# Two of thirty V loads cut into a 112-row transfer and sixteen loose rows from GpSimd's queue

## The chip, the core and the metric

One core of one Trainium2 chip runs the kernel. The core has five engines that work side by side: TensorE (PE, matrix products), VectorE (DVE), ScalarE (ACT), GpSimd (POOL) and SyncE (SP), which here only issues transfers. Data come from HBM into SBUF, the on-chip memory of 128 partitions, through 16 DMA engines that all issuing queues share. The metric is the device time of one execution in microseconds, lower is better; several executions are timed and their median is taken.

## The reference

One decode step of a gated mix: a grouped-query attention over a cached sequence of 65,536 keys, a small token-mixing network, and a gate between the two. What matters here is the attention, since it reads 536.9 MB of cache (8 heads x 65,536 x 256 x 2 bytes, for K and for V).

```python
def _A_ref(x, k_cache, v_cache, wq, wo):          # x [1,1,448], caches [1,8,65536,256], bf16
    q = (x @ wq).reshape(B, Sq, 16, 256)          # 16 query heads, two to each K/V head
    k = repeat(k_cache, 2, axis=1); v = repeat(v_cache, 2, axis=1)
    scores = einsum("bhqd,bhkd->bhqk", q, k) * 256 ** -0.5
    o = einsum("bhqk,bhkd->bhqd", softmax(scores), v)
    return o.reshape(B, Sq, 16 * 256) @ wo
g = sigmoid((x * gate_w).sum(-1))
out = g * _A_ref(...) + (1 - g) * _B_ref(...)     # _B_ref: layernorm, 448 x 1792 gelu network
```

## The kernel before

The cache is walked in 32 blocks, n = 0 to 31: four blocks of 16,384 positions for each of the 8 heads. In a block, partition p holds 128 neighbouring positions, so a row (one partition's share) of K or V is 128 x 256 numbers, 64 KB, and is contiguous in HBM.

Three buffers hold cache data. K of a block lies in two tiles, `kn0` and `kn1` (`k_tiles`, L79), each 128 rows of 32 KB; V lies in one tile `vt` (L80), 128 rows of 64 KB. There is no second copy of any of them: the next transfer into a buffer can begin only when the last reader of its old contents is done and the transfer before it into that buffer has landed.

A block does the following. `score_block` (L355) turns K around on TensorE (`transposes`, L332, four matrix transposes to a PSUM bank, then a copy by VectorE at L337) and multiplies it with the query (`scores`, L346). `softmax` (L394) takes the running maximum and exponentials. `products` (L490) multiplies the weights with V: four calls of `pv` (L369), one for each 32 of the 128 positions of a row, 16 matmuls each (L373), so calls 0 and 1 read the first half of each row of `vt` and calls 2 and 3 the second half. `accumulate` adds the result into `acc`.

All large loads are issued by SP, in program order: in block n first V of this block (`load_v`, L115, called at L527), then the two halves of K of the next block (`load_k`, L108). Each is one transfer of 128 rows. SP waits at V(n) until `products(n-1)` has read `vt`, and at each K half until `score_block(n)` has read that tile. `seq` (L58) keeps every engine's instructions in the order of the program; it orders only within an engine. GpSimd does four small things at the start of the kernel and nothing after that. Blocks 30 and 31 load V in smaller pieces, which the change leaves alone.

Names used below: V10 is V of block 10; K10a and K10b are the two halves of K of block 10. `KP` is 64, half of the 128 positions of a row; `VP` is 128.

## Time and profile before

| what | value |
|---|---|
| median of 3 timed runs | 1282.58 us (1281.82 to 1283.41) |
| the profiled execution's own time | 1282.07 us |
| its span, first to last instruction | 1280.3 us |
| PE busy | 980.6 us, 77% |
| DVE busy | 753.9 us, 59% |
| ACT, POOL busy | 43.0 us, 4.2 us |
| moved by DMA | 545.54 MB, mean 426 GB/s |
| issue to landing, K half (63 of them) | 26.8 us median |
| DVE's copy of a transposed K piece (L337) | 1024 x 0.685 us |
| TensorE's product with V (L373) | 1920 x 0.536 us |

The profile is one execution. A busy share says how much of the span an engine worked, not whether anything waited for it; the chain of waits and the waits of the issuing queue say that. The time from issue to landing counts what is still queued ahead of a transfer as well as its own time. The trace also keeps a record of every DMA packet with start, duration, size and queue, but not with the number of the DMA engine that carried it.

### The profile page before, as it was taken

The page shows a single profiled execution, that of the slowest core. Times are in us where ns is not written, and L with a number is a line of the kernel's source. Part 1 is how long each engine was busy: PE and PEld are TensorE (multiplying, and loading weights), DVE is VectorE, ACT ScalarE, POOL GpSimd, SP SyncE. Part 2 cuts the span into 40 slices and gives each one's busy share as a digit, 9 for nine tenths or more (in the row PEclk, how much of TensorE's full clock was granted, in tenths as well). Part 3 has the DMA queues.
Part 4 walks back from the last instruction along what each step waited for, and adds up shares of the span by engine and source line. Part 5 has one row for each costly group of instructions (what it writes and reads, how often), then busy time and mean ns, then how long its engine had stood idle before and what let it go on. Part 6 is the DMA issues. An engine that isn't in the chain of part 4 may idle for free.

```text
span 1280.3 us, 20506 instructions
## 1 busy us (share of the span) xinstructions
PE 980.6 (77%) x8941; PEld 643.2 (50%) x8941; DVE 753.9 (59%) x1368; ACT 43.0 (3%) x109; POOL 4.2 (0%) x7
## 2 busy tenths in 40 slices
PE   5777677787778787777876677866879777797797
PEld 4455444554545555445544455544456444565475
DVE  5465556664557655566654566644676545675573
ACT  4000000000000000000000000000000000000000
POOL 1000000000000000000000000000000000000000
PEclk9888878897888978889988889888888878897896
DMA  9999999999999999999999999999999999999897
GB/s 408 425 435 425 441 419 436 429 437 428 447 418 433 440 438 429 424 431 432 438 436 424 437 424 437 431 437 432 426 433 433 443 416 426 433 428 434 387 416 294
DMA packets 17716, 545.54 MB, mean 426 GB/s; under 512 B 2136, under 2 KB 4186, under 8 KB 4698
## 3 DMA queue, kind: packets, MB, share of 16 engines
q1 hardware_dynamic: 17188, 544.22, 98.8%
q8 instruction: 70, 1.15, 0.3%
q14 instruction: 20, 0.16, 0.0%
q10 hardware_dynamic: 438, 0.01, 0.0%
HBM read 544.22 MB, written 0.00 MB: 425 GB/s over the span
## 4 chain that ended last, share of the span: by engine, by line
DMA 67%; PE 30%; DVE 2%; issue 0%
DMA kn<-in_A_k_cache_dram 67%; PE tps L332 23%; PE sc_ps L346 5%; DVE kT L337 1%; PE pv_ps L387 1%; PE hd_ps L387 1%; DMA xr<-in_A_x_dram 0%; PE tps L589 0%; PE tps L554 0%; DVE rmax L398 0%; DVE z L280 0%; PE sm_ps L407 0%; DVE zt L279 0%; PE sm_ps L560 0%; PE sm_ps L496 0%
## 5 line engine op out<-in xcount | busy, mean ns | idle before, releaser
L337 DVE COPY kT<-tps 128x1024 bf16<-128x1024 bf16 x1024 | 646.5, 685 | 176.2 <-PE tps L332 175.2
L332 PE MATMUL tps<-ident_f,kn 128*128 128x128 f32 x4096 | 601.9, 296 | 99.7 <-DMA kn<-in_A_k_cache_dram 99.7
L332 PEld LDWEIGHTS tps<-ident_f,kn 128*128 128x128 f32 x4096 | 485.4, 150 | 219.1 <-DMA kn<-in_A_k_cache_dram 112.1
L373 PE MATMUL pv_ps<-vt,pT 128*4 128x512 bf16 x1920 | 172.1, 536 | 95.3 <-DMA vt<-in_A_v_cache_dram 89.5
L346 PE MATMUL sc_ps<-kT,qpad 128*32 128x512 bf16 x2048 | 201.1, 393 | 28.1 <-DVE kT L337 27.9
L373 PEld LDWEIGHTS <-pT 128*4 128x4 bf16 x1920 | 57.3, 110 | 197.4 <-issue 138.7
L439 DVE SCALAR_TENSOR_TENSOR acc<-acc,al,pv_ps 128x512 f32<-128x512 f32 x22 | 16.5, 748 | 163.0 <-PE pv_ps L373 163.0
L346 PEld LDWEIGHTS <-qpad 128*32 128x32 bf16 x2048 | 53.0, 93 | 110.7 <-issue 102.4
L416 ACT ACTIVATE p_sb<-sc_ps,nb 128x512 bf16<-128x512 f32 x32 | 22.0, 687 | 1205.5 <-DVE nb L410 1100.0
L444 DVE COPY acc<-pv_ps 128x512 f32<-128x512 f32 x8 | 5.5, 692 | 59.2 <-PE pv_ps L373 59.2
L429 DVE STREAM_TRANSPOSE pT<-p_sb 128x512 bf16<-128x512 bf16 x32 | 22.8, 711 | 28.3 <-ACT p_sb L416 28.3
L398 DVE TENSOR_REDUCE rmax<-sc_ps 128x1 f32<-128x512 f32 x32 | 22.1, 692 | 23.0 <-PE sc_ps L346 23.0
L399 PE MATMUL sm_ps<-ident_f,rmax 128*1 128x128 f32 x32 | 8.7, 271 | 25.4 <-DVE rmax L398 25.4
L407 PE MATMUL sm_ps<-mrun,ones_f 1*128 1x2 f32 x64 | 14.2, 288 | 14.1 <-DVE mrun L406 11.7
L399 PEld LDWEIGHTS sm_ps<-ident_f,rmax 128*1 128x1 f32 x32 | 2.5, 79 | 41.3 <-DVE rmax L398 41.3
L407 PEld LDWEIGHTS sm_ps<-mrun,ones_f 1*128 1x128 f32 x64 | 11.4, 221 | 20.2 <-DVE mrun L406 16.3
L410 DVE CUSTOM_DVE_ANT_0 junk<-sm_ps,nval 128x2 f32<-128x2 f32 x32 | 5.1, 159 | 17.1 <-PE sm_ps L407 17.1
L447 PE MATMUL hd_ps<-lsum,same 128*128 128x1 f32 x14 | 4.1, 362 | 13.9 <-DVE lsum L431 13.9
L447 PEld LDWEIGHTS hd_ps<-lsum,same 128*128 128x128 f32 x14 | 3.5, 310 | 14.5 <-DVE lsum L431 14.5
L400 DVE TENSOR_REDUCE mnew<-sm_ps 1x2 f32<-1x64 f32 x24 | 5.1, 212 | 8.7 <-PE sm_ps L399 8.7
L237 ACT ACTIVATE wo_sb<-h_bc,b1f,w1f 128x448 bf16<-128x448 f32 x14 | 9.2, 748 | 5.3 <-DVE h_bc L232 5.3
L461 PE MATMUL hd_ps<-esc,acc 128*128 128x2 f32 x28 | 4.4, 263 | 6.0 <-DVE acc L439 6.0
(107 smaller groups left out, 135.5 us busy)
## 6 DMA issues: line engine op xcount, KB each, us to landing
kn<-in_A_k_cache_dram SPq DMA_DIRECT2D x63, 4096.0 KB, 26.8
vt<-in_A_v_cache_dram SPq DMA_DIRECT2D x1, 5120.0 KB, 27.1
kn<-in_A_k_cache_dram SPq DMA_DIRECT2D x2, 2048.0 KB, 12.2
kn<-in_A_v_cache_dram SPq DMA_DIRECT2D x1, 4096.0 KB, 18.4
wo_sb<-in_A_wo_dram SPq DMA_DIRECT2D x1, 3584.0 KB
vt<-in_A_wq_dram SPq DMA_DIRECT2D x1, 3072.0 KB, 10.0
vt<-in_A_v_cache_dram SPq DMA_DIRECT2D x1, 3072.0 KB
kn<-in_A_v_cache_dram SPq DMA_DIRECT2D x1, 2048.0 KB, 17.9
```

Source lines behind the costliest of these rows:

```text
L237: seq(nc.scalar.activation(out=gel[:, b, :], in_=h_bc[:], func=ACT.Gelu_apprx_tanh, scale=w1f[:, b:b + 1], bias=b1f[:, b:b + 1],))
L332: seq(nc.tensor.transpose(tp[:, jj * 128:(jj + 1) * 128], k_tiles[i // 4][:, i % 4 * NJ + quarter * 4 + jj, :].bitcast(FP32), ident_f[:, :],))
L337: seq(nc.vector.tensor_copy(out=kT_tiles[i % 2][:, quarter * 4:(quarter + 1) * 4, :, :].rearrange("p j n c -> p (j n c)"), in_=tp[:, :].bi ...
L346: seq(nc.tensor.matmul(sc_ps[32 * a:32 * (a + 1), :], lhsT=qpad[:, c, g, i, :], rhs=kT_tiles[i % 2][:, :, 32 * a:32 * (a + 1), c], start=( ...
L373: seq(nc.tensor.matmul(pv_ps[32 * grp:32 * grp + 2 * REP, :, :], lhsT=pT[:, 32 * jj + 2 * REP * ip:32 * jj + 2 * REP * (ip + 1)], rhs=pair ...
L387: seq(nc.tensor.matmul(dst[:, c, :], lhsT=tile(j).rearrange("p (d c) -> p c d", c=2)[:, c, :], rhs=pT_tiles[v][:, 32 * jj + REP * i:32 * j ...
L398: seq(nc.vector.tensor_reduce(out=rmax[:], in_=sc_ps[:, :], op=ALU.max, axis=AXIS.X))
L399: seq(nc.tensor.transpose(sm_ps[0:1, 0:128], rmax[:, 0:1], ident_f[:, :]))
L407: seq(nc.tensor.matmul(sm_ps[:, 128:128 + REP], lhsT=ones_f[0:1, :], rhs=mrun[0:1, :], start=True, stop=True))
L416: seq(nc.scalar.activation(out=p_sb[:, :], in_=sc_ps[:, :], func=ACT.Exp, scale=scale, bias=nb[:, 0:1], accum_out=den[:, 0:1],))
L429: seq(nc.vector.transpose(out=pT[:, :], in_=p_sb[:, :]))
L439: seq(nc.vector.scalar_tensor_tensor(out=acc[:], in0=acc[:], scalar=al_tiles[n % 2][:, 0:1], in1=pv_ps[:, :, :], op0=ALU.mult, op1=ALU.add,))
```

## The change

In blocks 10 and 14, `load_v` is replaced by `load_v_rows`. It loads the first half of every row of V as one transfer from SP (128 rows of 32 KB). The second half comes as one transfer of rows 0 to 111 from SP, and rows 112 to 127 as small transfers issued by GpSimd: eight of two rows in block 10; one of three rows, six of two and one of one row in block 14. The one-row transfer is written by the compiler as 16 pieces of 2 KB, the others as whole rows of 32 KB. The bytes loaded, the place they land in and all arithmetic are the same.

```diff
+RH = 112
+ROWWISE = {10: (2,) * 8, 14: (3,) + (2,) * 6 + (1,)}
...
+    def load_v_rows(n):
+        load_v(n, 0, KP)
+        src = rows(A_v_cache, n)[:, KP:VP, :]
+        seq(nc.sync.dma_start(out=vt[0:RH, KP:VP, :], in_=src[0:RH]))
+        p = RH
+        for k in ROWWISE[n]:
+            seq(nc.gpsimd.dma_start(out=vt[p:p + k, KP:VP, :], in_=src[p:p + k]))
+            p += k
...
         if n < L - 1:
-            load_v(n)
+            (load_v_rows if n in ROWWISE else load_v)(n)
             load_k(n + 1, 0)
             load_k(n + 1, 1)
```

In the instruction streams, SP gains two transfers (two where there was one, in two blocks) and GpSimd gains sixteen; no other engine gains or loses an instruction. The waits move: the first of the sixteen transfers of each block waits, like SP's, for the products of the block before and for its V; the third call of `pv` in blocks 10 and 14 waits for nine transfers (the 112 rows and the eight small ones) before it may go on; and SP's next V load (V11, V15) waits for the landing of all ten pieces.

## The prediction

> **What bounds the kernel now.** First the page: the span, what the DMA engines did, the queues, the chain that ended last.

> ```profile
> span 1280.3 us, 20506 instructions
> DMA  9999999999999999999999999999999999999897
> q1 hardware_dynamic: 17188, 544.22, 98.8%
> q8 instruction: 70, 1.15, 0.3%
> q14 instruction: 20, 0.16, 0.0%
> DMA 67%; PE 30%; DVE 2%; issue 0%
> ```

> SP's transfers (queue 1) fill 98.8% of 16 DMA engines' time; PE is busy 77%. So the question is not what an instruction costs, but how much work lies on the DMA engine that is latest. The chain names PE for 30% because each load into a buffer waits for PE's reading of it. Whether that wait can idle the DMA engines is told by SP's own queue around block 10:

> ```profile
> start us, us, engine line op out<-in xcount [idle before <-releaser]
> 418.06 0.33 SPq L116 DMA_DIRECT2D vt<-in_A_v_cache_dram  x1
> 434.28 11.15 SPq L110 DMA_DIRECT2D kn<-in_A_k_cache_dram  x2
> 457.82 0.33 SPq L116 DMA_DIRECT2D vt<-in_A_v_cache_dram  x1
> ```

> and by the time to landing of the V loads around there, with the DMA engines' share in block 10:

> ```profile
> DMA to landing us min/median/max: 33.0/33.3/34.6
> ```

> ```profile
> 418.00:457.00 39.00, 29.41 (x255) 19.30 (x255) 23.08 (x40) 0.96 (x3) 0.00 (x0) 0.87 1.00 433
> ```

> (The last three numbers are PE's clock, the DMA share and GB/s.) V10 is issued at 418.06 and lands 33.2 us later, at 451.3. Its own work is 8 rows an engine at 2.418 us (median of the 3840 packets of 65,536 bytes in the record of packets), 19.3 us. So some 13 us of older work lay ahead of it: that is the cover under which a late issue costs nothing. DMA share 1.00 confirms it.

> Now the engines one by one. The record of packets names no engine, but each engine closes each transfer with a 4-byte packet, so every V load leaves 16 closing times. From it, in us of the span:

> ```
> load   early engines (7)      late engines (9)       latest behind earliest
> V1       97.50 to 99.26 (all 16)                      1.8
> V10     445.63 to 446.52      449.12 to 451.01       5.4
> V14     600.52 to 601.25      605.26 to 607.44       6.9
> V29    1183.32 to 1183.72     1190.95 to 1194.68    11.4
> ```

> All engines get the same rows, yet nine fall behind. Queue 8, the fetch of instructions, does it: its packets hold an engine 0.88 to 0.97 us each, come every 18 us, and return to the same engine every eighth time (the holes they leave in queue 1's packets show it); the ninth late engine carries queue 14, with 0.31 us holes. A transfer has landed when its latest engine is done, so the nine late engines set the time and the seven early ones have 4 to 11 us to give.

> **The change, part by part.** *Rows taken from SP's transfer.* 112 rows are 7 an engine in place of 8: each engine loses one row of 32 KB, 1.213 us (median of 8192 packets), in each of two blocks: -2.43 us on every engine. *Rows given back.* The 32 rows return through GpSimd's queue, 16 rows for 16 engines in each block. If each engine gets one, +2.43 us. This is the step on which all depends, and no row of this trace shows a small transfer of GpSimd. The trace has one queue of each kind: queue 8 takes turns over eight engines, queue 14 stays on one. I take turns, since the busier of the two (70 packets to 20) does so; eight transfers of two rows then cover 16 engines once. The other end is priced as a rival. [...]

> *Cutting V in two.* Two 32 KB packets take 2 x 1.213 against 2.418 us: +8 ns a row, 8 rows, +0.06 us a block; one more closing packet of 9 ns with 3 ns of gaps, +0.01 us. *Small transfers' own costs.* Closing packets: between one and eight more an engine and block, 0.01 to 0.10 us. A row moved in finer packets: between nothing and 16 x 0.084 - 1.213 = +0.13 us (the 2 KB packets of queue 1). Changing to another queue: queue 14's 8 KB took 0.309 us, as 8 KB on queue 1 do, so nothing; queue 8's 16 KB took 0.93 against 0.611 on queue 1, so up to +0.3 us; I take nothing, as queue 14's packets, like these, change only the queue, and queue 8's size is its own. Per block 0.08 to 0.60, taken 0.2; for two blocks +0.16 to +1.2, taken **+0.4 us**.

> *Issue.* SP gains two issues of 0.33 us, in a queue that waits 677 us for PE's reading of K: hidden, and with no cover 0.7 us. GpSimd has nothing else to do, and its rows pass what is queued on SP's rings, so they should be down long before the 33.2 us of the rest of V. The older K10b is held up by one row, 1.2 us, and with it the issue of K11b, under 13 us of cover (8 on the early engines). *Waits.* The third call of `pv` waits for nine transfers instead of one before the first call. Behind it on PE are block 11's transposes, for which SP's K12 loads wait. Since the first half of V lands some 9.7 us earlier, calls 0 and 1 (half of the 6.3 us that the 64 products of a block take) can run before the second half is there: PE waited 2.7 to 3.0 us for V in blocks 9 and 10, so the products end a little sooner or at the same time. SP's V11 and V15 wait for ten landings, all earlier than PE's last reading. All this only moves the cover; I count nothing.

> Sum for the profiled execution: 1282.07 + 0.4 = 1282.5 us; the median shown is 0.51 above it, so the predicted median is **1283.0**, its own range 1281.9 (the lowest run and the lower end of the costs) to 1284.6 (the highest and +1.2).

> **The rivals.** *B: the small transfers always start on the same engines (slower).* Then two engines take 7 + 8 rows in block 10 and again about as many in block 14: +7 x 1.213 = 8.5 us twice, 17.0 us, while the others are relieved. The place is the two engines' queue; it decides from the point where 8.5 us exceed their lead, and in block 10 the lead of an early engine is at most 5.4. An early pair ends 17.0 - 8.4 (the usual lead at V29, without the one straggler) = 8.6 later: 1291; a late pair 17 later: 1299.6. For it: queue 14 stays put. Against: queue 8, with the larger packets and more of them, moves on after each.

> *B2: turns, but uneven (slower).* If a late engine gets two rows in each block and another none, it gains 2 x 1.21 us: 1282.6 + 2.4 + 0.4 = 1285.4.

> *C: the rows fall on the early engines (faster).* The late ones then keep the relief, -2.43, less some of the 0.4: -2.0, so 1280.6. The most that 112 rows can bring is -2.43 + 0.15: 1280.3, short of 0.2% but for the spread of runs. For it: seven engines have the room. Against: turns reach early and late engines alike, and without turns two engines take all; seven of sixteen is neither.

> *D: GpSimd is slow to issue.* VectorE copies 32 x 0.686 = 22 us of each 38.6 us block; if GpSimd can prepare a transfer only beside that, eight at x us each end at 418.1 + 8x + about 3. Past x = 3.8 they are later than the rest of V; past 5.4 the cover of 13 us is gone too, and each further us costs 8 us a block: at 6 us, +10 us for both, 1293. The lower end is SP's 0.33 us an issue. [...]

> **How the numbers follow.** The likeliest is turns with one row each, 0.46: **1283.0**. C 0.18, B 0.16 (late pair 0.06 of it), B2 0.13, D 0.07. A difference of 0.2%, 2.6 us, is about what a measurement of this kernel can tell from no change. Faster by that: less than half of C, 0.08. Slower: B 0.16, most of B2 0.08, most of D 0.05, the outer edge of the likeliest 0.02: 0.31. Within: the rest, 0.61. The range goes from 1280.0 (all but the faster edge of C) to 1291.0 (an early pair); outside lie 0.08 below and about 0.09 above (late pair, part of D).

> **What would show it.** Turns: in the closing times of V10 and V14 of the changed kernel no group moves against the other by more than a packet, and K11a lands within 1.5 us of its old place against V9. B: two engines close K11a or V10 alone, some 3 us after the rest, and 10 us after V14. C: the late group comes 1.2 us nearer to the early one at each of the two blocks. D: GpSimd's transfers of block 10 are issued over more than 30 us, and PE's wait at `pv` in blocks 10 and 14 grows beyond 3 us. I am wrong altogether if the DMA share falls below 0.98 in a block where it was 1.00, since then the cover was not what I read.

## The result and the profile after

The changed kernel takes 1343.76 us (median of 4 runs, 1341.24 to 1344.94) against 1282.86 us (4 runs, 1281.82 to 1283.41): a ratio of 1.0472, 95% interval 1.0459 to 1.0484, so 60.9 us slower. The forecast was 1283.0 us with a range up to 1291.

First the page of the changed kernel (one profiled execution of 1342.58 us): the span, the DMA engines' share and rate in 40 equal slices of 33.5 us, the queues, the chain that ended last.

```profile
span 1340.8 us, 20547 instructions
DMA  9999999999999999999889999999999999999996
GB/s 419 415 428 439 431 433 432 422 435 434 434 435 399 229 350 402 432 420 300 280 357 412 433 414 434 429 431 431 440 437 427 432 427 431 432 438 434 400 390 277
q1 hardware_dynamic: 17444, 543.17, 97.3%
q0 software_dynamic: 512, 1.05, 0.4%
DMA 67%; PE 28%; another core or an unknown queue 3%; DVE 1%; issue 1%
```

The row of DMA shares looks like the one before, and the sum over queue 1 is 97.3% against 98.8%. The rate tells the two apart. The kernel before, in 40 slices of 32.0 us:

```profile
GB/s 408 425 435 425 441 419 436 429 437 428 447 418 433 440 438 429 424 431 432 438 436 424 437 424 437 431 437 432 426 433 433 443 416 426 433 428 434 387 416 294
```

In the changed kernel slices 14 and 15 (436 to 503 us, block 10) moved 229 and 350 GB/s, slices 19 to 21 (603 to 704 us, block 14) 300, 280 and 357, where the kernel before never falls below 416 GB/s from slice 2 to slice 37. GpSimd's own queue 0 carries 1.05 MB and holds the engines 0.4% of the time, some 5 us of the span if it were spread over all 16: far less than the loss.

SP's queue around block 10, in the changed kernel (start, duration, engine, line):

```profile
start us, us, engine line op out<-in xcount [idle before <-releaser]
416.55 0.33 SPq L118 DMA_DIRECT2D vt<-in_A_v_cache_dram  x1
419.37 0.34 SPq L123 DMA_DIRECT2D vt<-in_A_v_cache_dram  x1
434.10 14.33 SPq L112 DMA_DIRECT2D kn<-in_A_k_cache_dram  x2
488.96 0.33 SPq L118 DMA_DIRECT2D vt<-in_A_v_cache_dram  x1
```

and GpSimd's, the eight small transfers of block 10 and of block 14:

```profile
419.65 4.23 POOL L126 DMA_DIRECT2D vt<-in_A_v_cache_dram  x8 [414.94 <-PE pv_ps L384]
608.10 4.08 POOL L126 DMA_DIRECT2D vt<-in_A_v_cache_dram  x8 [184.22 <-PE pv_ps L384]
```

Everything of V10 has been issued by 423.9 us, as forecast, but V11 follows at 488.96 where it stood at 457.82 before. Nothing of V10 was late in being issued; it was late in landing. From the issues' table of the changed kernel, size and median time to landing of the V halves in blocks 10 and 14:

```profile
vt<-in_A_v_cache_dram SPq DMA_DIRECT2D x2, 4096.0 KB, 52.8
vt<-in_A_v_cache_dram SPq DMA_DIRECT2D x2, 3584.0 KB, 65.8
```

The whole of V landed in 33.3 us before; now half of it takes 52.8 and the 112 rows 65.8. PE's own timeline in block 10, with the idle time before each half of the products (two calls of `pv`) in brackets:

```profile
465.93 3.58 PE L384 MATMUL pv_ps<-vt,pT 128*4 128x512 bf16 x32 [14.53 <-DMA vt<-in_A_v_cache_dram]
485.33 3.59 PE L384 MATMUL pv_ps<-vt,pT 128*4 128x512 bf16 x32 [15.82 <-DMA vt<-in_A_v_cache_dram]
```

PE waits 14.53 us for the first half and 15.82 for the second, against 2.7 to 3.0 us in all before. What the DMA engines did meanwhile, by stretches (the last three numbers are PE's clock, the DMA share and GB/s):

```profile
418.00:437.00 19.00, 12.85 (x108) 9.22 (x100) 10.87 (x17) 0.00 (x0) 4.23 (x8) 0.89 1.01 377
437.00:472.00 35.00, 15.87 (x139) 9.25 (x139) 12.15 (x23) 0.96 (x3) 0.00 (x0) 0.76 1.02 227
472.00:485.00 13.00, 0.00 (x0) 0.00 (x0) 0.00 (x0) 0.00 (x0) 0.00 (x0) 0.55 0.95 351
485.00:492.00 7.00, 3.59 (x32) 0.98 (x32) 0.75 (x1) 0.00 (x0) 0.00 (x0) 0.50 0.77 297
```

This is the reading the forecast lacked. From 437 to 472 us all 16 engines are busy (share 1.02) and move 227 GB/s: each packet takes about twice as long. In the record of packets the median 32 KB packet takes 1.21 us before 434 us; half of those that start between 437 and 472 take 2.2 to 2.5 us, and 95% take 1.9 us or more. Sixteen packets are under way all that time, so this holds for all sixteen engines, those that are still in the first half of V or already in K11a among them. Only at the end (485 to 492) is there idle time, share 0.77: by then fewer and fewer engines have work (6 packets are under way at 488 us), SP cannot issue V11, and nothing is queued. Block 14 goes the same way and ends worse:

```profile
605.00:623.00 18.00, 14.02 (x126) 9.36 (x119) 10.04 (x16) 0.00 (x0) 4.08 (x8) 0.87 1.02 345
623.00:650.00 27.00, 12.73 (x89) 9.01 (x88) 9.31 (x15) 0.00 (x0) 0.00 (x0) 0.68 1.01 235
650.00:663.00 13.00, 6.57 (x59) 2.67 (x55) 4.05 (x11) 0.96 (x3) 0.00 (x0) 0.66 0.97 371
663.00:676.00 13.00, 3.58 (x32) 0.97 (x32) 0.32 (x1) 0.00 (x0) 0.00 (x0) 0.50 0.34 132
```

SP's queue there, before and in the changed kernel:

```profile
629.21 11.15 SPq L110 DMA_DIRECT2D kn<-in_A_k_cache_dram  x2
```

```profile
623.45 28.42 SPq L112 DMA_DIRECT2D kn<-in_A_k_cache_dram  x2
675.67 0.33 SPq L118 DMA_DIRECT2D vt<-in_A_v_cache_dram  x1
```

The lines marked x2 are each one group of two issues: K15b goes out 28 us behind K15a, where it was 11 before, because SP waits for PE's reading of K14b, and PE's timeline says what PE waited for there:

```profile
637.69 1.94 PE L343 MATMUL tps<-ident_f,kn 128*128 128x128 f32 x8 [14.27 <-DMA kn<-in_A_k_cache_dram]
```

K14b is older than V14 and has 128 rows; it is late all the same. The slow packets and GpSimd's rows on two of its engines can both have part in that; the trace does not separate them. From 665 us on engines run out of work: 9 packets are under way at 666, 4 at 668, 2 or 3 from 671 to 676.

Set against the kernel before's 432 GB/s, the bytes moved in each stretch say how much DMA time was lost: 2.4 us in 418 to 437, 21.9 in 437 to 500 (2.5 of it idle, 19.4 slow packets), 3.2 in 500 to 605, 27.6 in 605 to 690 (8.7 idle, 18.9 slow), 2.3 in 690 to 760. That is 57.4 of the 60.9 us, and some 45 of it are slow packets and not idle engines. In the kernel before the same stretches lose 0.1 us or less each.

One more thing stands in the record of packets. GpSimd's 32 KB packets of block 10 come two at a time: at 423.6 and 424.0, 429.4 and 429.9, 433.9 and 434.7, 440.1 and 442.4, 447.0 and 450.0, 454.4 and 457.0, 461.4 and 461.8, 466.8 and 469.6. Eight transfers issued within 4.2 us stand in line behind each other, two rows at once, as on two engines: a row takes 2.0 to 3.2 us and the next pair starts 4.5 to 7.7 us after the one before, which leaves room for SP's rows in between. In block 14 the one-row transfer's 16 pieces of 2 KB show two loaded engines from the other side: 14 pieces start between 635.9 and 643.0 us, the other two wait until 655.3 and 655.5, after the last row of the pairs.

The small packets of queue 0 bear on how such a transfer is dealt out. A two-row transfer leaves 32 packets there, two of 32 KB and 30 of 4 bytes. That would be two for each of 16 engines, with 14 shares empty; the packets carry no engine's number, so this is inferred from the count. A transfer of 16 rows from GpSimd, in the runs below, leaves 32 packets as well (64 for the two blocks).

So two things had to be told apart: what halves the rate, and what the stacking adds.

### The profile page after: what moved, and what is told of

Its sections match the earlier page's. It is cut to its first block, busy times and chain, and to the rows that moved or that the text cites. A ratio compares the mean times of both kernels' runs of the same rounds, so it can differ in the third digit from the quotient of the medians.

```text
span 1340.8 us, 20547 instructions
## 1 busy us (share of the span) xinstructions
PE 985.9 (74%) x8941; PEld 645.9 (48%) x8941; DVE 754.5 (56%) x1368; ACT 42.9 (3%) x109; POOL 12.5 (1%) x23
## 3 DMA queue, kind: packets, MB, share of 16 engines
q1 hardware_dynamic: 17444, 543.17, 97.3%
q0 software_dynamic: 512, 1.05, 0.4%
q8 instruction: 70, 1.15, 0.3%
HBM read 544.22 MB, written 0.00 MB: 406 GB/s over the span
## 4 chain that ended last, share of the span: by engine, by line
DMA 67%; PE 28%; another core or an unknown queue 3%; DVE 1%; issue 1%
DMA kn<-in_A_k_cache_dram 41%; DMA vt<-in_A_v_cache_dram 27%; PE tps L343 17%; PE pv_ps L384 5%; PE sc_ps L357 4%; DVE kT L348 1%; PE pv_ps L398 1%; PE hd_ps L398 1%; DVE rmax L409 0%; PE sm_ps L418 0%; DMA xr<-in_A_x_dram 0%; PE hd_ps L472 0%; PE tps L600 0%; PE tps L565 0%
## 5 line engine op out<-in xcount | busy, mean ns | idle before, releaser
L357 PE MATMUL sc_ps<-kT,qpad 128*32 128x512 bf16 x2048 | 201.6, 394 | 28.5 <-DVE kT L348 28.3
L440 DVE STREAM_TRANSPOSE pT<-p_sb 128x512 bf16<-128x512 bf16 x32 | 22.8, 711 | 28.3 <-ACT p_sb L427 28.3
L126 POOL DMA_DIRECT2D vt<-in_A_v_cache_dram x16 | 8.3, 527 | 599.2 <-PE pv_ps L384 599.2
## 6 DMA issues: line engine op xcount, KB each, us to landing
vt<-in_A_v_cache_dram SPq DMA_DIRECT2D x2, 4096.0 KB, 52.8
vt<-in_A_v_cache_dram SPq DMA_DIRECT2D x2, 3584.0 KB, 65.8
```

Of the source, the lines that this page charges most:

```text
L357: seq(nc.tensor.matmul(sc_ps[32 * a:32 * (a + 1), :], lhsT=qpad[:, c, g, i, :], rhs=kT_tiles[i % 2][:, :, 32 * a:32 * (a + 1), c], start=( ...
L440: seq(nc.vector.transpose(out=pT[:, :], in_=p_sb[:, :]))
```

## The experiments

In every run the first line of `load_v_rows`, the first half of V as one transfer, stays, and blocks 10 and 14 are changed unless said otherwise. The diffs show the lines that stand in place of those that load the second half in the changed kernel. A letter for a theory has the meaning that the expectation beside it gives. Runs without an interval are one execution, beside a kernel before of 1281.9 to 1283.9 us on the same chip.

### Two halves, full rows

```diff
+        load_v(n, KP, VP)
```

> V10 and V14 still come in two halves, but both halves as full transfers of 128 rows from SP; nothing from GpSimd. Theory R (the 112-row transfer is what is slow: 7 rows an engine instead of 8 put the 16 DMA engines in each other's way): the loss is gone, 1282 to 1284 us. Theory G (GpSimd's small transfers slow the DMA engines): also gone, 1282 to 1284. Theory C (cutting V in two is what costs, since PE waits in the middle of the products and V11 waits for both halves): 1320 to 1344 us.

Measured 1283.61 us (10 runs), ratio 1.0004, interval 0.9994 to 1.0013. Cutting V in two, with one more issue and 16 more closing packets a block, costs nothing that can be measured.

### The 112 rows alone, and with the other 16 from SP

```diff
+        seq(nc.sync.dma_start(out=vt[0:RH, KP:VP, :], in_=src[0:RH]))      # e3
```

> Leaves out rows 112 to 127 of the second half of V10 and V14 (they keep what was there), so one row of 32 KB an engine and block is not loaded, 2.4 us less work in all. Theory R: the 112 rows alone are slow, 1315 to 1342 us. Theory G: 1279 to 1283 us.

```diff
+        seq(nc.sync.dma_start(out=vt[0:RH, KP:VP, :], in_=src[0:RH]))      # e2
+        seq(nc.sync.dma_start(out=vt[RH:128, KP:VP, :], in_=src[RH:128]))
```

> The 112-row transfer stays; rows 112 to 127 come as one 16-row transfer from SP, none from GpSimd. Theory R: the loss stays, at least 1320 us, with packets of 32 KB at some 2.4 us while the 112 rows are under way. Theory G: the loss is gone, 1283 to 1288 us, packets at 1.2 us.

The 112 rows alone took 1310.99 us although they move less than the kernel before, and with the 16 rows from SP 1320.98. So 28 us of the loss need no GpSimd and no small transfer. The window from 439 to 457 us of the run with 112 rows alone:

```profile
439.00:457.00 18.00, 10.13 (x94) 5.45 (x93) 7.79 (x17) 0.96 (x3) 0.00 (x0) 0.88 1.01 218
```

Engines full, half the rate; the packets say the loss was 12.6 us in 437 to 500 and 14.0 in 605 to 690, with no idle time.

### GpSimd's queue, with the 112-row transfer taken away

```diff
+        seq(nc.gpsimd.dma_start(out=vt[:, KP:VP, :], in_=src))             # e5
```

> The whole second half of V10 and V14 as one GpSimd transfer of 128 rows, 8 an engine. A GpSimd queue that costs as such: at least 1290 us. If only row count and placement matter: 1281 to 1285 us.

```diff
+        seq(nc.sync.dma_start(out=vt[:, KP:96, :], in_=src[:, 0:32, :]))   # e4
+        for k in ROWWISE[n]:
+            seq(nc.gpsimd.dma_start(out=vt[p:p + k, 96:VP, :], in_=src[p:p + k, 32:64, :]))
+            p += k
```

> The second half of V10 and V14 has a 128-row transfer from SP for positions 64 to 95 and GpSimd's small transfers, as many and of the same rows, for positions 96 to 127 of rows 112 to 127. Leaves out positions 96 to 127 of rows 0 to 111: 4.2 us less work an engine and block. Theory G: GpSimd's transfers slow all engines, at least 1305 us. Theory R: no 112-row transfer, no loss, 1274 to 1280 us.

```diff
+        seq(nc.sync.dma_start(out=vt[:, KP:96, :], in_=src[:, 0:32, :]))   # e10
+        seq(nc.gpsimd.dma_start(out=vt[RH:128, 96:VP, :], in_=src[RH:128, 32:64, :]))
```

> As the run with 16 KB rows from GpSimd and no 112-row transfer (it leaves out the same part), but the 16 rows come as one GpSimd transfer instead of eight of two (or three, two, one). Theory S (every small transfer of GpSimd lands on the same two engines, one behind the other): one row an engine now, 1274 to 1277 us, some 4 to 6 less than the 1280.2 there. Theory G (the queue itself costs, whatever the engines): about 1280 again.

A full 128-row transfer through GpSimd's queue took 1283.79 us: that queue by itself costs nothing that one run can show. With small transfers beside 128-row ones (e4) the time was 1280.2 us, the half-rate stretch is gone (SP issues V11 at 456.85 us, at 457.82 before), and the small transfers again come in pairs about 3 us apart. Evenly spread they would have left 1274.1: 1282.7 less 2 blocks x 7 packets of 16 KB (8 fewer, one given back) x 0.611. The 6 us between fit two engines that keep their full load. The run with one 16-row transfer was to settle that and did not. At 1282.31 it missed the 1274 to 1277 of theory S, and from the 1280 of theory G it is 2 us away, which a single run does not tell from no difference (the ten runs with two halves lie 3.9 us apart). So this run does not show what the stacking costs. And 16 rows at once are slow in their own right:

```profile
418.00:437.00 19.00, 12.85 (x99) 10.11 (x96) 11.42 (x18) 0.00 (x0) 0.62 (x1) 0.90 1.00 368
```

Its 16 KB packets into rows 112 to 127 took up to 2.19 us instead of 0.61.

### The last 16 rows beside the 112, without stacking

```diff
+        seq(nc.sync.dma_start(out=vt[0:RH, KP:VP, :], in_=src[0:RH]))      # e11
+        seq(nc.gpsimd.dma_start(out=vt[RH:128, KP:VP, :], in_=src[RH:128]))
```

> The 112-row transfer stays, and the 16 loose rows come as one GpSimd transfer of 16 rows. Theory S: one row an engine, no stacking, 1312 to 1324 us. Theory G by number: one transfer in place of eight, also low, 1312 to 1324; a GpSimd queue that costs as such: at least 1335.

```diff
+ROWWISE = {10: (1,) * 16, 14: (1,) * 16}                                   # e12
```

> As the changed kernel, but GpSimd brings the 16 loose rows of each block as sixteen transfers of one row, each of which the compiler cuts into 16 pieces of 2 KB. Theory S (the part of the loss beyond the 112 rows comes from eight rows standing one behind the other on two DMA engines): a row is spread over 16 engines, so the loss shrinks to that of the run with 16 rows from SP, 1316 to 1326 us. Theory G (GpSimd's transfers cost by their number, whatever engine they land on): twice as many, so at least 1343 us.

1323.72 us for one 16-row transfer, 1326.24 for sixteen one-row transfers, each of which the compiler spreads over 16 pieces. Twice as many small transfers as in the changed kernel are 17.5 us cheaper, so the number of small transfers is not what is paid for. Queue 0 has 64 packets in the first run and 1024 in the second, 32 for each transfer, with 16 rows or pieces among them: one for each of 16 engines, if they are shared alike. Read so, the stacking costs 17.5 to 20 us by these two single runs.

### One block

```diff
+ROWWISE = {10: (2,) * 8}                                                   # e6
```

> Block 10 as in the changed kernel, block 14 as before. If the two blocks add up without touching each other, by the DMA work lost in the trace (26 us around block 10, 31 us around block 14): 1307 to 1312 us. If block 14 is worse because of what block 10 left behind (engines out of step): below 1305.

1307.25 us. Block 10 costs 24.6 us by itself. If the two blocks add up, block 14 costs the other 36; no run changes block 14 alone. The trace of the changed kernel has 8.7 us of idle engines around block 14 and 2.5 around block 10. Why block 14 costs more stays open.

### Is it the reading side?

The 112 rows are read from HBM 64 KB apart, like 128 rows. Two runs change only what is read, so the output is another.

```diff
+        flat = A_v_cache[0, g, b * BLK:b * BLK + RH * KP, :]               # e8: 112 rows, 32 KB apart
+        src = flat.rearrange("(p j) d -> p j d", j=KP)
+        seq(nc.sync.dma_start(out=vt[0:RH, KP:VP, :], in_=src))
```

> The 112 rows are written to the same places but read from other addresses: neighbouring rows 32 KB apart in HBM instead of 64 KB. Changes which positions are loaded, and leaves out the last 16 rows as the run with 112 rows alone did. Theory W (the loss is on the writing side): the same loss as there, 1305 to 1315 us, packets of 2.4 us. Theory H (the loss is on the reading side, from the distance between the engines' addresses): it changes with the distance, below 1300.

```diff
+        flat = A_v_cache[0, g, b * BLK:b * BLK + 128 * RH, :]              # e9: 128 rows, 56 KB apart
+        src = flat.rearrange("(p j) d -> p j d", j=RH)[:, 0:KP, :]
+        seq(nc.sync.dma_start(out=vt[:, KP:VP, :], in_=src))
```

> The second half of V10 and V14 as 128 rows written to their usual places, but read 56 KB apart, so that engines that are 8 rows apart read 448 KB apart, as in the 112-row transfer (7 rows of 64 KB). Changes which positions are loaded, not how many. Theory W: no loss, 1282 to 1285 us. Theory H: the loss of the 112 rows, at least 1300.

1310.6 us and 1282.34 us, with 216 and 436 GB/s between 439 and 457 us. Other addresses for 112 rows change nothing (1310.99 us and 218 GB/s before), other addresses for 128 rows cost nothing. So for 112 rows the half rate belongs to the rows that are written.

### Which rows a transfer writes

All of the second half is loaded in these runs, all by SP, in transfers of fewer rows.

```diff
+        seq(nc.sync.dma_start(out=vt[0:64, KP:VP, :], in_=src[0:64]))      # e7
+        seq(nc.sync.dma_start(out=vt[64:128, KP:VP, :], in_=src[64:128]))
```

> The second half of V10 and V14 as two transfers from SP, rows 0 to 63 and rows 64 to 127: four whole rows an engine in each, nothing from GpSimd. Theory W (16 engines can only run at full rate while they write all parts of the on-chip memory; a transfer that reaches half of the rows has half the ways in): both run at half rate, packets of 2.4 us, 1300 to 1315 us. Theory N (only a row count that does not give each engine 8 neighbours, or 7 in place of 8, is slow, because of odd counts): 64 is even, packets at 1.2 us, 1282 to 1285.

```diff
+        for h in range(2):                                                 # e13
+            seq(nc.sync.dma_start(out=vt[h::2, KP:VP, :], in_=src[h::2]))
```

> The second half of V10 and V14 as two transfers of 64 rows from SP again, but rows 0, 2, 4 ... and rows 1, 3, 5 ... instead of the lower and the upper 64. Theory P (what counts is which part of the 128 rows a transfer reaches: the lower or upper half has half the ways in, every second row has all of them): full rate, 1282 to 1286 us. Theory A (what counts is how rows are dealt to the engines: full rate only where each engine has its own 8 of 128 rows): slow like the two halves, 1300 to 1322 us.

```diff
+        seq(nc.sync.dma_start(out=vt[0:96, KP:VP, :], in_=src[0:96]))      # e15
+        seq(nc.sync.dma_start(out=vt[96:128, KP:VP, :], in_=src[96:128]))
```

> The second half of V10 and V14 as rows 0 to 95 (6 an engine) and rows 96 to 127 (2 an engine) from SP. Theory P: the 96 rows reach all parts as the 112 do, so they should not be slow for that, but the 32 rows reach a quarter of the rows, so 1285 to 1300 us. Theory A: both are slow, about as the 112 rows with 16 rows from SP (1321), 1312 to 1325 us.

1320.13 us for the two contiguous halves, 1282.56 for even and odd rows, 1323.05 for 96 and 32 rows. The same window for the three, in that order:

```profile
439.00:457.00 18.00, 10.63 (x99) 5.76 (x95) 8.15 (x17) 0.96 (x3) 0.00 (x0) 0.91 0.98 199
```

```profile
439.00:457.00 18.00, 13.85 (x135) 7.21 (x135) 9.12 (x20) 0.96 (x3) 0.00 (x0) 0.81 1.00 431
```

```profile
439.00:457.00 18.00, 10.84 (x99) 5.74 (x95) 8.14 (x17) 0.96 (x3) 0.00 (x0) 0.90 1.02 212
```

The first two both move 64 rows at a time in as many transfers: 199 GB/s for neighbours, 431 for every second row. Not the count decides, but which rows go together. The addresses that are read change along with the rows that are written here (neighbours in a transfer are 64 KB apart, or 128 KB), and for 64 rows no run parts the two. The 96 rows went against the simple form of that theory, by which they should have ended at 1300 us or less.

### Groups of rows

```diff
+            seq(nc.sync.dma_start(out=vt[h:RH:2, KP:VP, :], in_=src[h:RH:2]))   # e16, h = 0, 1
```

> The 112 rows of the second half come as two SP transfers of 56 rows, the even ones and then the odd ones; rows 112 to 127 of the second half of V are left out in blocks 10 and 14, as in the run with 112 rows alone (1311.0 us). Theory G (what counts is that the engines working at one moment write into different groups of eight neighbouring rows; a contiguous 112-row transfer deals 7 rows to an engine, so that two engines often meet in one group, while the even or odd rows are dealt four to an engine and keep each engine in its own group): the loss goes away, 1277 to 1285 us, with 32 KB packets of 1.2 us. Theory N (it is leaving out the last rows, or a transfer of fewer than 128 rows that ends at row 112, whatever the dealing): 1300 to 1313 us, with packets above 2 us.

```diff
+            seq(nc.sync.dma_start(out=vt[h:RH:2, KP:VP, :], in_=src[h:RH:2]))   # e17, h = 0, 1
+        for k in ROWWISE[n]:
+            seq(nc.gpsimd.dma_start(out=vt[p:p + k, KP:VP, :], in_=src[p:p + k]))
+            p += k
```

> The whole second half is loaded: 112 rows as 56 even and 56 odd ones from SP, and the same small GpSimd transfers as in the changed kernel (1343.8 us). Theory G: the part of the 112 rows (about 28 us of the 61) goes, the small transfers' own loss and their stacking on two engines stay: 1300 to 1317 us. Theory N: nothing is gained, 1335 to 1347 us.

```diff
+        for p in (0, 1, 64, 65):                                           # e18
+            seq(nc.sync.dma_start(out=vt[p:p + 63:2, KP:VP, :], in_=src[p:p + 63:2]))
```

> All 128 rows of the second half, as four SP transfers of 32 rows: rows 0, 2 .. 62, then 1, 3 .. 63, then 64, 66 .. 126, then 65, 67 .. 127. Theory G: each engine gets two rows of such a transfer, four neighbouring rows apart from the next engine's, so two engines always meet in one group of eight and half of the groups are idle: as slow as the two contiguous halves, 1305 to 1325 us with packets of 2.2 to 2.6 us. Theory E (any second row is enough, contiguous rows are the trouble): 1281 to 1286 us with packets of 1.2 us.

```diff
+        for h in range(8):                                                 # e20
+            seq(nc.sync.dma_start(out=vt[h::8, KP:VP, :], in_=src[h::8]))
```

> All 128 rows of the second half, as eight SP transfers of 16 rows, each of every eighth row (0, 8 .. 120, then 1, 9 .. 121, and so on), one row an engine. [...] Theory R (what counts is only that the rows of a transfer span all 128): 1282 to 1288 us, packets of 1.2 us.

1314.65 us (ratio 1.024, 1.021 to 1.0269), 1347.37 us (1.0494, 1.0446 to 1.0543), 1318.5 us (1.027, 1.024 to 1.0299), 1312.13 us (1.023, 1.02 to 1.026). The same window for the first and the third:

```profile
439.00:457.00 18.00, 10.30 (x95) 5.49 (x93) 7.93 (x17) 0.96 (x3) 0.00 (x0) 0.88 0.99 218
```

```profile
439.00:457.00 18.00, 10.62 (x99) 5.74 (x95) 8.15 (x17) 0.96 (x3) 0.00 (x0) 0.89 1.02 207
```

The idea that each engine needs only its own eight neighbouring rows fell with the first two: 56 even and 56 odd rows are as slow as 112 neighbours, and in the changed kernel they save nothing. The third says that every second row does not help while a transfer stays in one half of the rows (207 GB/s). The fourth says that spanning all 128 rows is not enough either:

```profile
439.00:457.00 18.00, 11.05 (x99) 5.75 (x95) 8.33 (x18) 0.96 (x3) 0.00 (x0) 0.91 0.97 207
```

## Why the prediction was wrong

**The mechanism, as far as the runs carry it.** What the runs show is that a packet's time depends on which rows its transfer, and the transfers beside it, carry; for 112 rows it is the rows written that count and not the addresses read (1310.6 and 1310.99 us). One engine's time for 32 KB is 1.213 us: the two-row transfers' packets take 2.0 to 3.2 us in the changed kernel, those of sixteen rows at once (the one 16-row transfer beside 112 rows) reach 4.6 to 4.7 us, 3.8 to 3.9 times 1.213. With two transfers of every second row, or one of all 128, the median packet between 439 and 457 us takes 1.21 us; with the other shapes of SP's transfers it takes 2.3 to 2.5. And the engines that work elsewhere, on K11a, slow down as well (2.2 to 2.5 us a packet).

The rates between 439 and 457 us put the shapes in two groups. The second half of each row as one transfer of 128 rows ran at 432 GB/s and even and odd rows at 431; the lower and upper halves ran at 199, the combs within a half and every eighth row at 207, 96 rows at 212, 112 rows and their even and odd ones at 218.

What stays open is what parts them. The "ways in" of theories W and P, and the rows that an engine gets of a transfer (7 of 112, four of the even rows), were the author's assumptions: the packets carry no engine's number, and no record names a way. Theory P missed the 96 rows (1323.05 us, 1285 to 1300 expected), theory A the even and odd rows (1282.56, 1300 to 1322) and theory G the 56 even rows (1314.65, 1277 to 1285).

**Step by step.** *What bounds the kernel.* Right: it is DMA-bound, and what was lost is DMA time. But I read the share as if it were throughput. The bytes and the DMA share together told the rate; a share of 1.02 at 227 GB/s did not occur to me as possible.

*Rows taken from SP's transfer* is the step that failed first. It priced 112 rows as 7 times the 1.213 us of a 128-row transfer's row, -2.43 us for both blocks. The row's price belonged to the transfer's shape: the 112 rows alone came to +28 us, at 2.2 to 2.5 us a row in place of 1.213, where all 16 engines were busy (share 1.01, 218 GB/s).

*Rows given back* failed in size and kind. Sixteen loose rows without stacking add 10 us (from SP), 12.7 (GpSimd, one transfer) or 15.2 us (GpSimd, sixteen transfers) to that, where I had +2.43 and 0.4 of small costs. Why they cost so much is not shown. Then "I take turns" was wrong: the transfers stand in line two rows at a time, as on the same two engines, and no run shows turns among GpSimd's transfers; which two engines these are, no run shows either. Queue 14, which stays on its engine, was the nearer row, and queue 8 was not.

The three parts are differences of one run after the other, so they add up as they must: 28.3 for the 112 rows, 12.7 to 15.2 for the loose rows from GpSimd, 17.5 to 20.0 for the stacking, 61 in all.

*Rival B* (0.16) named that mechanism and its place, and its price was still short: 8.5 us per block by 1.213 us a row gave 1291 or 1299.6, but a stacked row took 2.0 to 3.8 us, with SP's rows of 2.4 between one pair and the next. The stacking itself cost 17.5 to 20 us, near the 17.0 that B has for a late pair, but with packets that took twice B's price the agreement is partly luck; what B lacked is the rest. *C* and *B2* need the rows on more than two engines and fall with that. *D* fell: the eight issues took 4.2 us, 0.52 each, far below 3.8. That GpSimd has nothing else to do and issues early was right, and its first rows did pass what SP had queued: they started at 423.6 us, while PE got the first half of V10, issued 3.1 us before them, at 465.9. That its rows would be "down long before" the rest of V was wrong, as the last one started at 469.6 us, 46 us after the last issue had ended.

*Cutting V in two*: right, +0.14 us forecast for both blocks, nothing measurable found. *Waits*: I counted on the cover of 13 us. It was real and was used up: V10 landed at 485.3 us in place of 451.3, PE waited 30 us for it, and with PE late, V11, K15b and V15 were issued late, which is the idle part of the loss (11 of 57 us).

*What would show it.* The bound given there, a DMA share below 0.98 in a block, was met (0.97 over block 10, from 418 to 489 us, and 0.88 over block 14, from 605 to 676), but that shows a small part of the loss; the rate in GB/s, 289 and 269 over the same stretches, shows the whole. A wait of PE at `pv` beyond 3 us was given as a sign of D; it came (30 us in block 10) without D, so it could not tell D from a slow transfer.

**The weights.** Every case that was weighed took the durations of packets as fixed and moved only their number, their engine or their time of issue. No row of the profile before could give the price of a 112-row transfer, since all large loads there have 128 rows. That was a reason to bound the cost from above by something far larger than 1.2 us a block, and I did not give it one.

## What to carry to other kernels

In a kernel that lives on DMA rate, these runs speak for large SBUF loads of all 128 rows and, if they have to be cut, for a cut along the row (1283.6 us) or into even and odd rows (1282.6), not for leaving some rows out (1311.0) or for halves of the rows (1320.1): 112 rows ran at 218 GB/s where 128 ran at 432, and in the changed kernel packets of K11a beside them took 2.2 to 2.5 us in place of 1.21. Read GB/s beside the DMA share, because a share of 1.0 here went with 227 GB/s as well as with 432. Small transfers from GpSimd did not spread by themselves here: two rows stood in line behind two rows eight times running, from 423.6 to 469.6 us.
